# The gate's two weight loads cut into 120 and 8 partitions, in a one-core linear-attention and highway kernel

## The chip, the core and the metric

The kernel runs on one core of a Trainium2 chip. The metric is the device time of one execution in microseconds (us). A time shown for a kernel is the median of its runs. A profile is one execution recorded by the hardware profiler; its "span" is the part from the first to the last recorded instruction.

## What is computed

```python
# q, k, v: (8, 8, 576, 64) f32; w_h, w_t: (512, 512) f32; b_t: (512,) f32
q_s = exp(q - max) / sum            # softmax over the 64 of a head
k_s = exp(k - max) / sum            # softmax over the 576 positions
kv  = einsum('bhsd,bhse->bhde', k_s, v)
x   = einsum('bhsd,bhde->bhse', q_s, kv)   # then (8, 8, 576, 64) -> (4608, 512)
H = maximum(x @ w_h, 0)
T = 1 / (1 + exp(-(x @ w_t + b_t)))        # the gate
out = T * H + (1 - T) * x
```

The output is 4608 x 512 in f32. `w_t` is what is called the gate's weights here.

## The kernel before

**Stages.** For each of the eight batches the kernel loads k, v and q (1152 KB each), takes exponentials on ScalarE (ACT; L252 for k, L301 and L306 for q), casts v to f16 (L258, on GpSimd, ACT or VectorE), and multiplies k by v on TensorE (PE, L268). The result, divided by its row sums (L280, L286), stays in SBUF as weights. q is transposed on PE (L318, L323), copied back (L332) and multiplied by these weights (L352); VectorE (DVE) divides by the sums (L361, L367), which gives a tile x of 128 tokens by 512. There are 36 such tiles. Each is transposed (L375, L382) and multiplied by both weight matrices, four products of 128x512 each: with w_t into the gate's bank (L402) and with w_h (L410). Tanh on ACT (L424, L426), a maximum on DVE (L430), and two or three operations on GpSimd (POOL) or DVE (L441, L442, L444, L462) give the output, which is stored in pieces of 128 to 512 KB (L470, L478, L482).

**The order** is written out by hand: `ORDER`, a list of some 680 steps. A step's name says what it does and for which batch or tile; a letter after the colon picks the engine. Each engine runs its instructions in the order in which the steps issue them. Near the change the list has these loads, in this order, all on the queue of SyncE (SP): `w_h_0`, `w_h_2`, `w_t_2`, `w_t_0`, `k_1_2`, `v_1_2`, `q_1_0`, `k_1_0`, `v_1_0`, `q_1_4`, `q_2_0`, `k_2_0`, `v_2_0`, `q_3_0`. The number after the letter is the batch; the last number is the column group from which the piece starts (for w_t_2 and w_t_0 it names the half of the matrix).

**A weight load** (`load_w`, L207 to L210) brings half a matrix: 128 partitions with two rows of 512 f32 each, 4096 bytes per partition and 512 KB in all. w_h's halves are lessened by an identity on POOL (L225) and cast on ACT (L231). w_t's halves are cast on POOL (`wt_cast`, L221), w_t_2 first and w_t_0 after it. A product with w_t (L402) needs both halves.

**The queue.** A transfer of the program is spread over the core's 16 DMA engines; each engine works through its share of the transfers in the order of issue. The program has eight semaphores for transfers, taken in turn: a transfer is issued only once the eighth transfer before it has landed. A landing counts when every engine that carries a part has reported.

The lines that a load of the weights is made of:

```python
T[f"w{w}{c}"] = op.tile([P, 2, DM], FP32, tag="o32", name=f"w32{w}_{c}")
nc.sync.dma_start(T[f"w{w}{c}"], src.rearrange("(c p r) n -> c p r n", p=P, r=2)[c // 2])
...
copy(w16["t"][:, c:c + 2], T[f"wt{c}"])        # wt_cast, on POOL here
```

Of the kernel before, what the change touches and what calls it, by code (L numbers as in the profile page):

```python
# [65 lines left out]
def kernel(  # L66
# [10 lines left out]
    nc = tc.nc  # L77
    B, H, S, D = q.shape
    DM = H * D
    P = 128  # L80
# [36 lines left out]
    T = {}  # L117
# [89 lines left out]
    def load_w(e, w, c):  # L207
        src = dict(t=moe_w_t, h=moe_w_h)[w]
        T[f"w{w}{c}"] = op.tile([P, 2, DM], FP32, tag="o32", name=f"w32{w}_{c}")
        nc.sync.dma_start(T[f"w{w}{c}"], src.rearrange("(c p r) n -> c p r n", p=P, r=2)[c // 2])  # L210

    def load_b(e, r):
        nc.scalar.dma_start(b32[r:r + 1], moe_b_t.rearrange("(o n) -> o n", o=1))
# [250 lines left out]
    def st(e, i, h):  # L464
# [20 lines left out]
    does = dict(  # L485
        setuppool=setup_pool, setupdve=setup_dve, bsplit=bsplit, fill=fill,
        k=load_kv("k"), v=load_kv("v"), q=load_q, w=load_w, b=load_b, bp=bp, bc=bc,
        wtc=wt_cast, whc=wh_cast, whd=wh_less_identity, ek=ek, vc=vc, kv=kv, kr=kr, kn=kn, eq=eq, qt=qt, qc=qc,
        xu=xu, rs=rs, x=x, xt=xt, xe=xe, bw=bw, mt=mt, mh=mh, th=th, dd=dd, uu=uu, oo=oo, st=st)
# [35 lines left out]
```

## Time and profile before

| | |
|---|---|
| median of three runs | 119.56 us (119.36 to 119.63) |
| the profiled execution's own time | 119.67 us |
| its span | 117.6 us, 3461 instructions |
| PE busy | 110.6 us (94% of the span) |
| DVE, ACT, POOL busy | 94.3, 92.3, 91.9 us (80%, 78%, 78%) |
| DMA | 40.06 MB in 22083 packets, mean 341 GB/s |
| the chain that ended last, by engine | PE 69%, DMA 17%, DVE 8% |
| w_t loads, issue to landing | 2 x 512 KB, 11.2 us each |

Matmuls are pipelined, so a busy PE is not one at its peak. The chain that ended last is followed back from the last instruction: at each step to what released it, or to the instruction before it on its engine. A share of DMA in it means that the engines waited for transfers at that place. Besides the instructions the trace holds, for each transfer, the time at which each DMA engine's report arrived (called marks below: 16 for a transfer over 16 engines), and every DMA packet with its start, duration and size; it doesn't say which DMA engine a mark or a packet belongs to.

### The profile page before, as it was taken

The numbers are of one execution on the slowest core, as the hardware profiler recorded it, in microseconds if no ns is written. First come the engines' busy times: TensorE is split into PE (matmuls) and PEld (weight loads), VectorE is DVE, ScalarE is ACT, GpSimd is POOL, SyncE is SP. The second block draws the span as 40 slices with busy tenths as digits, with TensorE's granted clock in tenths as the row PEclk, the third lists the DMA queues.
The fourth block names the chain that finished last, engine by engine and source line by source line (L and its number), as shares of the span: only waits on it lengthen the run. The fifth ranks groups of instructions, "written<-read, shape, count | busy, mean of one in ns | idle before, by whom it ended". The sixth has DMA issues, their size and how long they took to land.

```text
span 117.6 us, 3461 instructions
## 1 busy us (share of the span) xinstructions
PE 110.6 (94%) x1371; PEld 63.6 (54%) x1371; DVE 94.3 (80%) x223; ACT 92.3 (78%) x130; POOL 91.9 (78%) x103
## 2 busy tenths in 40 slices
PE   5999867989999999999999999999999999999991
PEld 1354443535655666556655566666666655554450
DVE  5654685588769899997899999889989898988870
ACT  4375481798999999799999999996998987774520
POOL 5022237299999999999999999899999789996860
PEclk9999999999999999999999999999999999999999
DMA  2999999999999999999999999999999977971595
GB/s 46 393 392 380 408 396 385 378 375 384 394 389 390 389 391 362 374 355 390 389 375 383 381 363 361 395 374 380 406 403 363 279 235 180 301 283 56 210 364 173
DMA packets 22083, 40.06 MB, mean 341 GB/s; under 512 B 3250, under 2 KB 9650, under 8 KB 22068
## 3 DMA queue, kind: packets, MB, share of 16 engines
q1 hardware_dynamic: 21920, 39.72, 94.8%
q8 instruction: 10, 0.16, 0.6%
q10 hardware_dynamic: 148, 0.14, 0.4%
q14 instruction: 5, 0.04, 0.1%
HBM read 30.41 MB, written 9.44 MB: 339 GB/s over the span
## 4 chain that ended last, share of the span: by engine, by line
PE 69%; DMA 17%; DVE 8%; SPq 2%; ACT 1%; issue 1%; DVEq 0%
PE gps L410 23%; PE tps L402 22%; DMA q<-in_q_dram 11%; PE xu L352 6%; DMA v<-in_v_dram 6%; PE turned L375 5%; PE kv L268 4%; DVE x L367 4%; PE qps L323 2%; PE qps L318 2%; SPq L183 2%; PE turned L167 2%; DVE d L430 2%; ACT qe L306 1%; DVE rs L361 1%
## 5 line engine op out<-in xcount | busy, mean ns | idle before, releaser
L462 POOL TENSOR_TENSOR o<-u,x 128x512 f32<-128x512 f16 (+1 forms) x36 | 40.7, 1144 | 3.7 <-DVE u L444 2.8
L402 PE MATMUL tps<-w16t,xT 128*128 128x512 f16 (+1 forms) x148 | 36.3, 373 | 0.8 <-POOL w16t L221 0.8
L410 PE MATMUL gps<-w16h,xT 128*128 128x512 f16 x144 | 36.3, 379 | 0.0
L367 DVE TENSOR_TENSOR x<-xu,rs 128x512 f16<-128x512 f32 (+1 forms) x39 | 25.2, 649 | 2.8
L442 POOL TENSOR_TENSOR u<-g,d 128x512 f16<-128x512 f16 x21 | 24.3, 1157 | 2.5 <-DVE rs L361 0.9
L430 DVE SCALAR_TENSOR_TENSOR d<-x,gps 128x512 f16<-128x512 f16 x36 | 24.2, 678 | 1.7 <-PE gps L410 1.6
L252 ACT ACTIVATE ek<-k 128x576 f16<-128x576 f32 (+2 forms) x15 | 18.0, 1222 | 2.5 <-DMA k<-in_k_dram 2.5
L402 PEld LDWEIGHTS <-xT 128*128 128x128 f16 x148 | 13.4, 98 | 12.1 <-issue 1.1
L410 PEld LDWEIGHTS <-xT 128*128 128x128 f16 x144 | 12.8, 98 | 11.4 <-DVE xT L382 0.5
L390 ACT COPY tps<-ball 128x512 f32<-128x512 f32 x28 | 16.3, 592 | 2.4 <-DVE u L444 2.1
L258 POOL CAST v<-v 128x1152 f16<-128x1152 f32 (+1 forms) x10 | 9.5, 953 | 10.4 <-DMA v<-in_v_dram 9.9
L375 PE MATMUL turned<-idh,x 128*128 128x128 f16 x144 | 14.3, 220 | 1.0 <-DVE x L367 1.0
L352 PE MATMUL xu<-kvb,eq 128*128 128x130 f16 (+1 forms) x160 | 14.8, 224 | 0.5 <-DVE eq L332 0.2
L167 PE MATMUL turned<-blank 128*128 128x512 f16 x44 | 12.5, 431 | 1.3 <-POOL blank L149 1.3
L352 PEld LDWEIGHTS <-eq 128*128 128x128 f16 (+1 forms) x160 | 10.2, 100 | 6.5 <-DVE x L367 1.3
L424 ACT ACTIVATE th<-tps 128x512 f16<-128x512 f32 x21 | 12.3, 592 | 1.6 <-PE tps L402 1.6
L375 PEld LDWEIGHTS <-x 128*128 128x128 f16 x144 | 10.1, 98 | 6.5 <-DVE x L367 2.6
L441 POOL TENSOR_SCALAR g<-th 128x512 f16<-128x512 f16 x21 | 13.1, 622 | 0.2 <-ACT th L424 0.2
L382 DVE COPY xT<-turned 128x512 f16<-128x512 f16 (+1 forms) x27 | 10.8, 399 | 2.8 <-PE turned L375 2.5
L306 ACT ACTIVATE qe<-q 128x1024 f16<-128x1024 f32 (+2 forms) x8 | 9.2, 1160 | 4.3 <-DMA q<-in_q_dram 4.1
L426 ACT ACTIVATE tps<-tps 128x512 f32<-128x512 f32 (+1 forms) x16 | 8.9, 556 | 2.9 <-PE tps L402 2.7
L444 DVE SCALAR_TENSOR_TENSOR u<-tps,d 128x512 f16<-128x512 f32 (+1 forms) x15 | 10.0, 669 | 0.8 <-ACT tps L426 0.2
(48 smaller groups left out, 114.6 us busy)
## 6 DMA issues: line engine op xcount, KB each, us to landing
k<-in_k_dram SPq DMA_DIRECT2D x6, 1152.0 KB, 11.6
v<-in_v_dram SPq DMA_DIRECT2D x6, 1152.0 KB, 14.4
out_dram<-o SPq DMA_DIRECT2D x23, 256.0 KB, 6.3
q<-in_q_dram SPq DMA_DIRECT2D x10, 512.0 KB, 9.5
out_dram<-o SPq DMA_DIRECT2D x6, 512.0 KB, 5.5
k<-in_k_dram SPq DMA_DIRECT2D x4, 576.0 KB, 11.9
q<-in_q_dram SPq DMA_DIRECT2D x2, 1152.0 KB, 15.6
q<-in_q_dram SPq DMA_DIRECT2D x2, 640.0 KB, 10.5
```

The source lines that it names most:

```text
L167: nc.tensor.matmul(spare, blank[:, 0:P], blank, start=True, stop=True, skip_group_check=True)
L252: nc.scalar.activation(t[:, :, c:c + n].rearrange("p j c d -> p c j d"), T[f"k32{b}"][:, c:c + n].rearrange("p c (j d) -> p c j d", j=NJ), ...
L352: nc.tensor.matmul(dst, turned_q(b, jp, n), kvb[b % NKV][:, hh, kk], start=True, stop=True, skip_group_check=True)
L367: nc.vector.tensor_mul(t[:, k0:k1], sums(i, k)[:, :, :, 0:64], T[f"rs{i}_{k}"][:, 0:k1 - k0].unsqueeze(3).to_broadcast([P, k1 - k0, 4, D]))
L375: nc.tensor.matmul(t[:, n], T[f"x{i}"][:, n0 + n % 2:n0 + 2 * P:2], idh, is_transpose=True, start=True, stop=True, skip_group_check=True)
L390: nc.scalar.copy(t[:, cs], ball[:, cs])
L402: nc.tensor.matmul(T[gate(i, k)][:, cs], T[f"xT{i}"][:, n], w16["t"][:, n, cs], start=False, stop=(n == parts[-1] and not first), skip_gro ...
L410: nc.tensor.matmul(t, T[f"xT{i}"][:, n], w16["h"][:, n], start=(first and n == parts[0]), stop=(n == parts[-1] and not (first and len(part ...
L430: nc.vector.scalar_tensor_tensor(t, T[f"x{i}"], -0.5, T[f"gps{i}"], op0=ALU.mult, op1=ALU.max)
L441: nc.gpsimd.tensor_scalar(g, T[f"th{i}"], 1.0, 1.0, op0=ALU.add, op1=ALU.mult)
L442: nc.gpsimd.tensor_mul(t, g, T[f"d{i}"])
L462: eng.tensor_add(t[:, cs], T[f"u{i}_{h}"][:, cs], T[f"x{i}"][:, cs])
```

## The change

`load_w` issues each load of w_t as two transfers to the same tile: one of partitions 0 to 119 and one of partitions 120 to 127. The loads of w_h stay whole. The tile, its consumers and `ORDER` are the same; two transfers are added to SP's queue, so that each later transfer takes the semaphore two places further on. Each cast of w_t waits for two transfers.

```diff
     def load_w(e, w, c):
         src = dict(t=moe_w_t, h=moe_w_h)[w]
         T[f"w{w}{c}"] = op.tile([P, 2, DM], FP32, tag="o32", name=f"w32{w}_{c}")
-        nc.sync.dma_start(T[f"w{w}{c}"], src.rearrange("(c p r) n -> c p r n", p=P, r=2)[c // 2])
+        rows = src.rearrange("(c p r) n -> c p r n", p=P, r=2)[c // 2]
+        for part in (slice(0, 120), slice(120, P)) if w == "t" else (slice(0, P),):
+            nc.sync.dma_start(T[f"w{w}{c}"][part], rows[part])
```

## The prediction

> **What bounds the kernel now.** I read the slices and queues first.
>
> ```profile
> DMA  2999999999999999999999999999999977971595
> ...
> q1 hardware_dynamic: 21920, 39.72, 94.8%
> q8 instruction: 10, 0.16, 0.6%
> ```
>
> The DMA engines are full from the fourth microsecond to about 90 us, so a load lands when the engines get to it, not when it is issued. The q8 row is PE's own instructions: ten fetches of 16 KB; 0.6% of 16 engines' 117.6 us is 1.1 us for each, and each is one packet on one engine. Next, the waits and the chain:
>
> ```profile
> ACT qe L306 <- DMA q<-in_q_dram: 4.1, 4, 1.9
> ...
> POOL w16t L221 <- DMA w32t<-in_moe_w_t_dram: 1.9, 2, 1.6
> ...
> PE tps L402 <- POOL w16t L221: 0.8, 1, 0.8
> ```
>
> ```profile
> 3.79 7.00 DMA v<-in_v_dram
> 10.81 12.67 DMA q<-in_q_dram
> ...
> 23.50 1.06 ACT qe L306
> 24.56 0.05 issue
> 24.61 0.62 PE qps L323 x8
> ```
>
> Up to q_1_0's landing at 23.47 transfers set the end; from 24.6 the chain is PE, with DVE in two stretches, to the end. So an early landing before 23.5 pays, if no later landing takes it back. The marks show what lands last (last three of 16, us):
>
> ```
> w_h_2  15.05 15.06 15.15     k_1_2  19.10 19.22 20.45     q_2_0  30.02 31.24 31.38
> w_t_2  16.33 16.43 17.64     q_1_0  22.11 22.22 23.47     v_2_0  36.80 37.24 37.39
> w_t_0  17.60 17.70 18.95     q_1_4  26.93 27.04 28.26
> ```
>
> One engine falls behind in w_t_2 and stays 1.2 to 1.25 us behind the next. A q8 packet starts at 15.15 and takes 1.10 us: call its engine **the late one**. The fetch at 26.95 makes a second engine late, from q_2_0 on. The last of the others (16.43, 22.22) is the one that carried the one-row bias loads: the second bias row stood in its queue from 3.74 to 4.44, and one engine alone ended the transfer around it 0.7 us later than the rest.
>
> **The change part by part.** *Price of a row.* A 4096-byte packet takes 0.16 us around 15 us. 128 rows on 16 engines are 8 rows each, 1.28 us; w_h_2's first mark to w_t_2's is 1.25. How 120 rows are shared out no trace here shows. Nearest to the row "8 on each of 16" is 8 on each of 15, which leaves one engine out; I take that. The other bound is 15 rows on each of 8 engines. The 8 rows are one each on 8 engines, at most one row on any of them: 0.16 us per load, 0.33 for both with their marks (none, for an engine that gets none). The engine left out saves 16 rows, 2.56 us, more than the 1.54 us by which the late one missed its own slot (17.64 against 16.10).
>
> [...]
>
> *New landings, if the late engine is the one left out.* The bias engine, with its extra rows, is last: w_t_2 at 16.43 + 0.17 = 16.60 (17.64 now), w_t_0 at 17.70 + 0.33 = 18.03 (18.95), k_1_2 19.55 (20.45), q_1_0 22.22 + 0.33 = 22.55 (23.47): 0.92 earlier.
>
> *PE up to 31 us.*
>
> ```profile
> 17.69 1.04 POOL L221 CAST w16t<-w32t 128x1024 f16<-128x1024 f32 x1 [1.59 <-DMA w32t<-in_moe_w_t_dram]
> 19.00 1.04 POOL L221 CAST w16t<-w32t 128x1024 f16<-128x1024 f32 x1 [0.27 <-DMA w32t<-in_moe_w_t_dram]
> ```
>
> ```profile
> 18.24 1.03 PE L410 MATMUL gps<-w16h,xT 128*128 128x512 f16 x4
> 20.09 1.89 PE L402 MATMUL tps<-w16t,xT 128*128 128x512 f16 x8 [0.83 <-POOL w16t L221]
> ```
>
> The second cast would run from 18.08 to 19.12; PE is free at 19.27 (18.24 + 1.03), so the gate's first products start there instead of at 20.09: 0.82 gained, the wait of 0.8 above. The exponential of q_1_0 then follows 22.55 instead of 23.47, and PE's transposes 0.92 before 24.61. PE carries 0.92 onwards.
>
> *What takes it back.* q_2_0 and v_2_0 land with the second late engine, which nothing relieves: 31.38 and 37.39 stay.
>
> ```profile
> 31.40 2.12 ACT L306 ACTIVATE qe<-q 128x2304 f16<-128x2304 f32 x1
> 33.43 1.07 ACT L424 ACTIVATE th<-tps 128x512 f16<-128x512 f32 x2
> 34.38 1.11 ACT L390 COPY tps<-ball 128x512 f32<-128x512 f32 x2
> 35.42 2.13 ACT L252 ACTIVATE ek<-k 128x2304 f16<-128x2304 f32 x1
> 37.44 1.14 ACT L258 CAST v<-v 128x1152 f16<-128x1152 f32 x1
> ```
>
> ```profile
> 37.51 1.15 POOL L258 CAST v<-v 128x1152 f16<-128x1152 f32 x1
> ```
>
> ACT was free at 31.26 and starts at 31.40, behind the landing; from there it has no gap. The casts of v_2_0 end at 38.58 (ACT) and 38.66 (POOL) whatever came before, and PE's k-by-v products of batch 2 need both. They start at 38.98 in the chain (38.91 in PE's own rows). With 0.05 for the handover, as from the cast's end 20.04 to 20.09, they can't start before 38.71: **0.27 us is left** of 0.92. The next such place is v_3_0: its casts end at 47.69, the products start at 48.03, 0.34 less the 0.05 is 0.29, enough. After that no landing stands in the chain.
>
> *Costs at nothing.* SP issues two more transfers, 0.33 us each by L210's rows, and each transfer behind them waits for a landing two places later: q_1_0 issues after w_h_0's landing at 13.88, not at 10.81; k_1_2 at 10.8, not 8.54. Behind them on SP stand only later loads. The cover is the backlog: q_1_0's share starts on the engines no earlier than 19.6 (v_1_2's first mark, 20.10, less some 0.5 from an engine's last packet to its mark), 5.7 us after its issue, while the first load of the program had its first packet 1.1 us after issue. Without that cover each microsecond of late issue would be one of landing. Each cast waits for two transfers: one semaphore more, 0 to 0.1 us, hidden before PE's 19.27 (0.15 of room).
>
> *Sum.* The profiled execution's own 119.67 (117.6 span and 2.07 around it) would become 119.40; the median shown lies 0.11 lower, so 119.56 - 0.27 = **119.29 us**.
>
> **The rivals.** The trace doesn't number engines, so which one is late decides. For the forecast: the late engine isn't the bias engine, which took the 16.43 mark; each of the fetches up to 53.3 (five) hits another engine, and none hits the bias engine as far as the marks can be followed. One after the other is the simplest such order. [...] Against it: a walk may start anywhere, and any of 15 engines fits the mark.
>
> *R1, slower.* The late engine is one of the eight that get a row more. Place: q_1_0's last mark, 23.47 + 0.33 = 23.80, and w_t_0's, 18.95 + 0.33, so PE starts both the gate's products and the transposes 0.33 later, and the later landings (31.24 + 0.33 = 31.57) don't give it back. 119.89 us. It decides as soon as the late engine carries any of the 8 rows. [...] In this trace no engine lags but after a fetch.
>
> *R2, no effect.* The late engine is one of the others that keep 8 rows: 17.64, 18.95 and 23.47 stay and the extra rows hide in 1.2 us of lag. 119.56.
>
> *R3, eaten.* The late engine is relieved, but the second late one is among the eight: v_2_0 at 37.72, casts to 38.99, products at 39.04 against 38.98. 119.62.
>
> *R4, the split doesn't do what it says.* 15 rows on 8 engines are 2.4 us for each load instead of 1.28: 1.12 twice, and the row more, 2.57 on 22.22 is 24.79, 1.3 later; on the late engine 2.6. Some 2 us, 121.56.
>
> **How the numbers follow.** Forecast 0.45, R1 0.22, R2 0.18, R3 0.11, R4 0.04. 0.2% is 0.24 us, about what a measurement of this kernel can tell from no change. The forecast has bounds of 0 and -0.92 and lies near the line: 0.30 of its 0.45 faster, 0.15 same. R1: 0.18 slower, 0.04 same. R2: 0.14 same, 0.02 to each side. R3: 0.08 same, 0.03 slower. R4 slower. Faster 0.32, same 0.41, slower 0.27. The range goes from 119.00 (0.56 gained, half-way between 0.27 and 0.92 and a little less) to 119.95 (R1 and 0.06); R4 and the outer parts of the others are outside, under 0.2. Alone, the forecast's own range is 119.00 to 119.50.
>
> **What would show it.** Right: fewer than 16 marks of data for a 120-row load, last mark of w_t_2 near 16.6 and of q_1_0 near 22.55, the gate's first products at 19.3, the exponential of q_2_0 still at 31.4, and the k-by-v products of batch 2 at 38.7. R1 would show q_1_0 at 23.8, R2 at 23.47, R3 the products at 39.0, R4 the first mark of w_t_0 after 18.5. Wrong altogether would be a gap in the DMA slices before 31 us, from SP's later issues.

## The result

The changed kernel takes **122.86 us** (median of 4 runs, 122.33 to 123.15) against 119.50 us for the kernel before in the same rounds (119.36 to 119.63): a ratio of 1.0276, 95% interval 1.0237 to 1.0316. It is slower by 3.4 us; the forecast was 119.29 and its range ended at 119.95. The profiled execution took 122.72 us with a span of 120.9 (119.67 and 117.6 before). Two executions of one experiment below, the 60, 60 and 8 split, were disturbed (123.6 and 123.7 us) and are left out of its figures. All line numbers from L210 on are two higher than before: the casts of w_t are L223, the gate's products L404.

The page of the changed kernel, three rows by slices of 3.0 us (the granted clock of PE, the busy share of the DMA engines, and what they moved):

```profile
PEclk9999999769999999999999999999999999999999
DMA  2999999999999999999999999999999957970595
GB/s 51 395 395 383 377 232 249 372 385 378 385 394 388 398 380 378 362 365 384 383 384 371 393 358 372 386 371 379 399 406 353 283 196 199 299 285 7 220 381 173
```

The GB/s row of the kernel before, in slices of 2.9 us:

```profile
GB/s 46 393 392 380 408 396 385 378 375 384 394 389 390 389 391 362 374 355 390 389 375 383 381 363 361 395 374 380 406 403 363 279 235 180 301 283 56 210 364 173
```

The DMA row has a 9 in each slice from the second to the 32nd, up to 96 us: the engines do not run dry. But in the sixth and seventh slice, 15 to 21 us, busy engines move 232 and 249 GB/s; before they moved 396 and 385. That is where the pieces of w_t are loaded. The same traffic is slower, and a row of busy shares cannot show it.

The waits of the changed kernel, in us in total, times and the longest:

```profile
POOL w16t L223 <- DMA w32t<-in_moe_w_t_dram: 4.1, 2, 2.6
...
PE tps L404 <- POOL w16t L223: 3.2, 1, 3.2
```

The casts now wait 4.1 us for w_t (1.9 before), and PE waits 3.2 us for the second cast (0.8 before). The casts on POOL and the products on PE in order of time:

```profile
19.29 1.04 POOL L223 CAST w16t<-w32t 128x1024 f16<-128x1024 f32 x1 [2.63 <-DMA w32t<-in_moe_w_t_dram]
21.75 1.04 POOL L223 CAST w16t<-w32t 128x1024 f16<-128x1024 f32 x1 [1.42 <-DMA w32t<-in_moe_w_t_dram]
```

```profile
18.61 1.03 PE L412 MATMUL gps<-w16h,xT 128*128 128x512 f16 x4
22.84 3.49 PE L404 MATMUL tps<-w16t,xT 128*128 128x512 f16 x8 [3.21 <-POOL w16t L223]
```

The first products of the gate start at 22.84 (20.09 before), and the eight take 3.49 us instead of 1.89: behind the long wait PE's granted clock is 0.5 from 22.96 to 26.37 us (a mean of 0.7 and 0.6 in the eighth and ninth slice of the PEclk row), and the products follow one another every 0.43 us instead of 0.216. The group's row has it too, 37.9 us busy and a mean of 386 ns (36.3 and 373 in the kernel before, whose clock stays full):

```profile
L404 PE MATMUL tps<-w16t,xT 128*128 128x512 f16 (+1 forms) x148 | 37.9, 386 | 3.2 <-POOL w16t L223 3.2
```

And the chain that ended last, by engine and then its part from 3 to 30 us:

```profile
PE 56%; DMA 15%; ACT 11%; POOL 8%; DVE 3%; SPq 2%; issue 1%; DVEq 0%; POOLq 0%
...
3.25 6.74 DMA k<-in_k_dram
10.00 11.63 DMA w32t<-in_moe_w_t_dram
21.75 1.05 POOL w16t L223
22.84 3.49 PE tps L404 x8
26.33 0.30 PE turned L377 x4
26.63 0.88 PE gps L412 x4
...
27.54 0.69 DVE d L432
28.22 0.09 DVE rz L282
...
28.37 1.16 POOL u L444
```

Before, it went through q_1_0's landing and ACT to PE at 24.6; now it goes through the landing of w_t. Instruction by instruction, PE in the changed kernel stands 2.75 us behind before at the first gate product, 4.43 at 22 to 23 us (of before), 3.64 from 26 to 60, and 3.43 from 80 us to the end. Some 0.8 us is given back at 24.6, where PE waited 0.57 us for q_1_0 before and does not wait now, and 0.2 later. The rest stays. Behind 22 us the chain holds no transfer: its two loads make 18.4 us, the whole 15% of DMA, and what follows is work of PE, DVE, POOL and ACT with hardly a gap. The loads that follow are late too, since they stand behind the slow packets in the same queues: the last mark of q_1_0 is 25.86 (23.47 before), of q_2_0 33.95 (31.38).

Packets and marks come straight from the trace. The 256 packets of 4096 bytes that load w_t last as follows:

```
               150-180 ns  180-220  220-260  260-300  300-340  over 340   mean
before                254        0        0        0        0         2    164
after                  36       40       37       41       47        55    273
```

### The profile page after: what moved, and what is told of

The parts are those of the page before. It is cut to its first block, busy times and chain, and to the rows that moved or that the text cites. A ratio compares the mean times of both kernels' runs of the same rounds, so it can differ in the third digit from the quotient of the medians.

```text
span 120.9 us, 3465 instructions
## 1 busy us (share of the span) xinstructions
PE 112.0 (93%) x1371; PEld 64.1 (53%) x1371; DVE 94.5 (78%) x223; ACT 92.0 (76%) x130; POOL 91.7 (76%) x103
## 4 chain that ended last, share of the span: by engine, by line
PE 56%; DMA 15%; ACT 11%; POOL 8%; DVE 3%; SPq 2%; issue 1%; DVEq 0%; POOLq 0%
PE tps L404 20%; PE gps L412 19%; DMA w32t<-in_moe_w_t_dram 10%; DMA k<-in_k_dram 6%; PE xu L354 5%; PE turned L377 5%; ACT ek L254 3%; PE kv L270 3%; POOL u L444 3%; POOL o L464 3%; PE qps L320 2%; PE turned L167 2%; ACT v L260 2%; ACT tps L392 2%; ACT qe L308 2%; SPq L183 2%
## 5 line engine op out<-in xcount | busy, mean ns | idle before, releaser
L404 PE MATMUL tps<-w16t,xT 128*128 128x512 f16 (+1 forms) x148 | 37.9, 386 | 3.2 <-POOL w16t L223 3.2
L412 PE MATMUL gps<-w16h,xT 128*128 128x512 f16 x144 | 36.3, 379 | 0.0
L404 PEld LDWEIGHTS <-xT 128*128 128x128 f16 x148 | 13.7, 100 | 15.3 <-issue 5.1
```

The lines of the kernel that those rows point to most:

```text
L404: nc.tensor.matmul(T[gate(i, k)][:, cs], T[f"xT{i}"][:, n], w16["t"][:, n, cs], start=False, stop=(n == parts[-1] and not first), skip_gro ...
L412: nc.tensor.matmul(t, T[f"xT{i}"][:, n], w16["h"][:, n], start=(first and n == parts[0]), stop=(n == parts[-1] and not (first and len(part ...
```

## The experiments

The theories, from the two traces. **P**, place: what counts is where in SBUF the packets of a piece go; the pieces make several DMA engines write into the same group of partitions. **E**: a transfer over 15 engines is slow as such. **H**: the order of the rows in the source memory counts. **S** and **Q**: the small piece as such, or the place of the extra transfers in the queue. **C**: of the 3.4 us a good part is PE's clock, which is at 0.5 behind the wait.

Each diff below is against the changed kernel unless it says otherwise, and its lines are in `load_w`; lines that only allocate a tile or register a step are not shown. The kernel before had medians of 119.53 in the rounds of the first four kernels, 119.79 for the next four, 119.75 for the 60, 60 and 8 split and the repeat of the changed kernel, and 119.66 for every fourth and every eighth partition. The mean duration of w_t's packets and the marks are of the profiled execution.

**Two halves of 64 neighbouring partitions.**

```diff
-        for part in (slice(0, 120), slice(120, P)) if w == "t" else (slice(0, P),):
+        for part in (slice(0, 64), slice(64, P)) if w == "t" else (slice(0, P),):
```

> Each w_t load as partitions 0 to 63 and 64 to 127. All 16 engines carry both pieces, 4 rows each. Theory P (destinations): a piece of neighbouring partitions, as it is shared out, puts several engines on the same group of SBUF partitions at once, and their packets slow each other. P expects rows as slow as in the changed kernel (some 0.3 us instead of 0.16), w_t_0 landing at 21 to 22 us and 122 to 123 us in all. Theory E (engine count): it is the 15 engines, or their uneven load, that is slow; E expects packets of 0.16 us, w_t_0 landing near 18.9 and 119.5 us. Theory S (the small piece): single rows on 8 engines hold up the queue; S expects 119.5 too. [...]

121.75 us (121.16 to 122.13), ratio 1.017 (1.0132 to 1.0209); packets 269 ns; w_t_0's last mark 21.04. All 16 engines take part, and the packets are as slow as in the change. E alone can't be the cause, nor the small piece. The time lies a little under the 122 to 123 that P expected; the halves lose 2.2 us where the change loses 3.4.

**The same halves, but even and odd partitions.**

```diff
-        for part in (slice(0, 120), slice(120, P)) if w == "t" else (slice(0, P),):
+        for part in (slice(0, P, 2), slice(1, P, 2)) if w == "t" else (slice(0, P),):
```

> Each w_t load as its 64 even and its 64 odd partitions. All 16 engines, 4 rows each, two transfers as in e1. The wide q loads of the kernel before have the same stride of two and took 1.47 to 1.50 us for 512 KB, as the whole-partition load q_1_0 did (1.49). P expects little or no slowing (every piece reaches all of the partitions' groups): w_t_0 near 19 to 19.5, 119.4 to 120. E and S expect 119.5. A time like the changed kernel's, 122 to 123, would say that it is the number of transfers, or of rows per engine, and not the destinations.

119.58 us (118.94 to 120.41), ratio 0.9995 (0.9963 to 1.0026); packets 164 ns; w_t_0 18.96, q_1_0 23.47, the marks of before to 0.01. The GB/s rows of the two kernels, halves first:

```profile
GB/s 47 382 396 378 385 241 283 372 384 377 390 392 389 393 385 375 364 363 382 387 384 368 393 359 369 386 383 374 404 400 387 272 200 180 280 327 12 216 381 174
```

```profile
GB/s 47 388 396 379 405 399 383 377 377 387 389 391 392 388 392 359 375 354 389 390 374 383 379 365 361 396 373 380 406 403 372 333 158 219 327 231 39 216 369 178
```

Two transfers of 64 rows each in both, issued in the same places: 241 and 283 GB/s against 399 and 383 in the same slices. The second transfer, its issue and the casts' second wait cost nothing that can be measured (the interval ends at 0.3 us).

**112 and 16 partitions.**

```diff
-        for part in (slice(0, 120), slice(120, P)) if w == "t" else (slice(0, P),):
+        for part in (slice(0, 112), slice(112, P)) if w == "t" else (slice(0, P),):
```

> Each w_t load as 112 and 16 partitions. All 16 engines carry both, 7 rows and 1 row each, so that no engine has more or less work than before. E expects no loss: 119.5. S expects little (the small piece is spread over 16). P expects most of the loss of the changed kernel, since seven neighbouring rows for each engine again cross the groups: packets of 0.25 to 0.3 us in the larger piece and 121 to 123 us.

121.69 us (120.86 to 122.56), ratio 1.0171 (1.0113 to 1.0229); packets 250 ns. Again 16 engines, again slow.

**The whole load, and the 8 rows once more** to a tile that nobody reads.

```diff
-        for part in (slice(0, 120), slice(120, P)) if w == "t" else (slice(0, P),):
-            nc.sync.dma_start(T[f"w{w}{c}"][part], rows[part])
+        nc.sync.dma_start(T[f"w{w}{c}"], rows)
+        if w == "t":
+            nc.sync.dma_start(scratch[120:P, c // 2], rows[120:P])
```

> Each w_t load whole, and behind it a second transfer of the 8 last rows, to a tile that nothing reads. S expects most of the loss: w_t_0 late by 1 us or more and over 121 us, and so would a cost of the two added places in the queue. P and E expect the price of the rows alone: at most 0.33 us on eight of the engines, 119.5 to 119.9.

120.32 us (119.96 to 121.36), ratio 1.0075 (1.0039 to 1.011). Neither expectation held, 119.5 to 119.9 or over 121. The 8 rows alone cost 0.8 us, more than the 0.33 of their bytes; the mean packet is 182 ns, and 50 of the 272 last over 180 ns, where before had 2 of 256.

**The same with the 8 rows four partitions apart** (the diff is against the kernel just above).

```diff
-            nc.sync.dma_start(scratch[120:P, c // 2], rows[120:P])
+            nc.sync.dma_start(scratch[0:32:4, c // 2], rows[120:P])
```

> e3 (each w_t load whole, and 8 rows more to a tile that nothing reads), with the 8 rows now to partitions 0, 4, ... 28 instead of 120 to 127. P expects that the 8 rows go to eight groups of partitions and disturb little: the price of rows, 0 to 0.33 us, 119.5 to 119.9, against 120.3 in e3. Theory Q (a place in the queue or the second transfer as such costs 0.8) expects 120.1 to 120.5 again.

119.61 us (119.34 to 119.85), ratio 0.9992 (0.9959 to 1.0024); 270 of 272 packets between 150 and 180 ns. The same rows of the source and the same number of bytes and transfers: the 0.8 us were their destinations. S and Q fall. The forecast's 0.33 for the added rows is more than enough for these destinations, and too little for those of the change.

**Source and destination crossed**, one execution of each. Here the rows of the gate's matrix land in other places, so its products are of a matrix with moved rows. Only the added lines of the diffs are shown; they stand for w_t's loads alone.

```diff
+            nc.sync.dma_start(T[f"w{w}{c}"][0:64], rows[0:P:2])
+            nc.sync.dma_start(T[f"w{w}{c}"][64:P], rows[1:P:2])
```

> Destinations as in e1 (partitions 0 to 63, then 64 to 127), sources as in e2 (every other row of the matrix): the gate's weights lie in the wrong partitions, so the gate is that of a matrix with its rows moved. Theory P (destinations) expects packets as slow as e1's, a mean of 250 to 280 ns, w_t_0's last mark past 20.5 and 121 to 122.5 us. Theory H (sources: engines that read neighbouring rows of the matrix hinder each other in memory) expects e2: 164 ns, 19.0, 119.5 us.

```diff
+            nc.sync.dma_start(T[f"w{w}{c}"][0:P:2], rows[0:64])
+            nc.sync.dma_start(T[f"w{w}{c}"][1:P:2], rows[64:P])
```

> The reverse: destinations every other partition as in e2, sources in neighbouring halves as in e1; the gate's matrix has its rows moved here too. P expects e2: a mean of 164 ns for a packet and 119.5 us. H expects e1: 270 ns, 121 to 122.5 us.

Destination halves from alternate source rows: 121.94 us, packets 275 ns. Alternate destinations from source halves: 119.91 us, packets 164 ns. In the GB/s rows, the halves first:

```profile
GB/s 51 391 394 379 387 232 282 371 388 377 389 390 389 387 392 374 362 364 380 392 384 365 395 357 369 386 381 374 403 401 383 320 172 222 315 251 29 219 363 175
```

```profile
GB/s 42 359 395 381 405 397 387 376 376 384 392 391 389 386 391 364 370 359 386 394 371 384 377 365 363 398 370 382 404 400 366 310 164 225 325 237 37 209 376 178
```

The slow slices (232 and 282) go with the destination, whatever the source. H falls.

**The changed kernel with PE kept busy** through its wait: 14 products of a zero tile are added into an open bank, behind the product with w_h that ends at 19.9 us.

```diff
- ... mh_3_0 qc_0_2:A ...
+ ... mh_3_0 z_14 qc_0_2:A ...
+    def zeros(e, n):
+        for _ in range(n):
+            nc.tensor.matmul(T[gate(1, 0)], blank[:, 0:P], blank, start=False, stop=False, skip_group_check=True)
```

> The changed kernel with 14 products of zeros added into the gate's bank of tile 1 before its first products, so that PE doesn't stand still while it waits for the cast; the sums are the same. Theory C (the wait of 3.2 us makes the granted clock fall, and the gate's first eight products run at half speed, 3.5 us instead of 1.7) expects the granted clock at 0.99 or more, these products at 1.7 to 1.9 us, and 122.86 less 0.4 to 1.2: 121.7 to 122.4 us. If the landings alone set the end, 122.7 to 123 stays.

A miss: 123.08 us (122.93 to 123.33), ratio 1.0289 (1.0246 to 1.0331). The clock did stay up (a mean of 1.0), and the timeline of PE shows the products:

```profile
19.72 3.18 PE L173 MATMUL tps<-blank 128*128 128x512 f16 x14
23.39 1.89 PE L408 MATMUL tps<-w16t,xT 128*128 128x512 f16 x8 [0.49 <-POOL w16t L227]
```

The eight products take 1.89 us again, and from 31 to 60 us this execution is 0.73 ahead of the changed kernel, though its first gate product starts 0.55 later. Its chain goes through q_1_0's landing, as before the change, and reaches PE's transposes 2.94 us later than there (24.61):

```profile
14.11 12.30 DMA q<-in_q_dram
...
26.44 1.07 ACT qe L312
...
27.55 0.62 PE qps L329 x8
```

At 69 us it falls back, from 0.73 ahead to 0.27 behind:

```profile
68.14 0.70 PE L274 MATMUL kv<-v,ek 64*64 64x65 f16 x62
69.64 0.28 PE L274 MATMUL kv<-v,ek 64*64 64x65 f16 x10 [0.80 <-issue]
```

PE stops for 0.80 us in the middle of one batch's k-by-v products, 62 of 72 done, and waits for nothing that the profile names. A fetch of PE's instructions ran from 67.24 to 68.32, just before. The 14 products are 28 more instructions, each with its weight load as the 1371 of both on the page of the changed kernel, so the fetches fall at other places of the program; in the changed kernel the fetch nearest to this place (67.90 to 69.01) stops nothing. That the fetch is the cause was not tried. So C holds in part: the fallen clock is worth some 0.7 us at 60 us, and this way of keeping it up costs more than that later. The four executions of the changed kernel itself point the same way: the one whose mean granted clock was 1.000 had a span of 120.5 us, the three at 0.986 had 120.7 to 120.9. By these two comparisons the clock is 0.2 to 0.7 of the 3.4 us.

**60, 60 and 8 partitions**, the 120 as even and odd.

```diff
-        for part in (slice(0, 120), slice(120, P)) if w == "t" else (slice(0, P),):
+        for part in (slice(0, 120, 2), slice(1, 120, 2), slice(120, P)) if w == "t" else (slice(0, P),):
```

> The 120 rows of the change as two transfers of 60, even and odd partitions of the first 120, and the last 8 as before in a transfer of their own: still one engine left out of 15, but every engine's four rows lie on alternate partitions, as in the split into even and odd that took no longer than the whole load. Theory P (the slow packets come from pieces of neighbouring partitions that several engines write at once): the packets of the 60 rows near 164 ns; the 8 neighbouring rows may still cost what the 8 extra rows cost, 0.8 us; so a mean below 200 ns, last mark of w_t_0 at 18.9 to 19.9, time 119.3 to 120.4. If 15 engines instead of 16 are slow as such: packets of 250 ns or more and 122 us or more. If the forecast was right in its mechanism and only the packets' price spoilt it (the engine left out is the late one): last mark of w_t_2 near 16.6 and q_1_0 near 22.55 in the traced execution, and about 0.3 us under the kernel before, 119.3; if the late engine is not the one that is left out, nothing is gained.

A miss: 121.98 us (121.35 to 122.12), ratio 1.016 (1.0107 to 1.0213), packets 238 ns. The partitions of each piece alternate, and it is slow. That 15 engines are slow as such, for which 250 ns and 122 us or more were expected, would fit this run almost as well; it does not separate the two, and the slow kernels that speak against E are those with 16 engines. "Pieces of neighbouring partitions" was the wrong wording of P. What would fit is that engines can get in each other's way also when the rows of a piece alternate.

This gives a wider theory, **P2**: what counts is how many engines write to one group of partitions at the same moment. Which partitions make a group, and which engine writes which row, no trace here shows; there P2 rests on the author's assumption. The last two kernels test it with steps of four and of eight partitions.

**Every fourth partition, four transfers of 32 rows.**

```diff
-        for part in (slice(0, 120), slice(120, P)) if w == "t" else (slice(0, P),):
+        for part in [slice(i, P, 4) for i in range(4)] if w == "t" else (slice(0, P),):
```

> Each load of the gate's weights in four transfers of 32 rows, every fourth partition. [...] With two rows for each of 16 engines. [...]

Two outcomes were expected, by how the rows of a piece are dealt to the engines: 164 ns a packet and 119.2 to 120.3 us if the engines keep apart, 250 to 300 ns and about 121.7 us if two of them meet. If the number of transfers is what costs, the time was to be more than 0.5 us above the even and odd split with either. The packets are as fast as whole (mean 165 ns, 244 of 256 between 150 and 180). The time is not: 120.99 us (120.31 to 121.89), ratio 1.0109 (1.0054 to 1.0163). Stretches of 1 us show why (busy time of each engine with its instructions in brackets, and at the end PE's clock, the DMA share and GB/s):

```profile
16.00:17.00 1.00, 0.74 (x7) 0.41 (x7) 0.79 (x4) 0.78 (x2) 0.64 (x2) 1.00 0.80 307
17.00:18.00 1.00, 0.43 (x8) 0.43 (x9) 0.85 (x2) 0.99 (x2) 0.00 (x0) 1.00 0.54 155
18.00:19.00 1.00, 1.00 (x10) 0.53 (x8) 0.42 (x1) 0.00 (x0) 0.82 (x1) 1.00 0.86 170
19.00:20.00 1.00, 1.00 (x9) 0.52 (x8) 0.89 (x4) 0.37 (x1) 0.76 (x2) 1.00 1.00 382
```

Here the DMA share does fall, to 0.54, with fast packets: the engines run dry. SP issues the eight pieces from 7.57 to 16.18 us, because from the fourth on most wait for a landing, and k_1_2 follows at 16.22 (10.76 in the changed kernel). Six more issues cost some 0.9 us on q_1_0's landing (24.40, before 23.47). The packets are those of the first outcome, the time is not: at 1.0109 of the kernel before, against 0.9995 for the even and odd split, the number of transfers does cost here, by their issues.

**Every eighth partition, eight transfers of 16 rows**, for w_t_2 alone; w_t_0 whole; one execution.

```diff
-        for part in (slice(0, 120), slice(120, P)) if w == "t" else (slice(0, P),):
+        for part in [slice(i, P, 8) for i in range(8)] if (w, c) == ("t", 2) else (slice(0, P),):
```

> Only the first load of the gate's weights (w_t_2) in eight transfers of 16 rows, every eighth partition; w_t_0 whole. [...] P2: the 128 packets of w_t_2 take 250 to 300 ns, those of w_t_0 164, so a mean of some 210 to 230 over both; w_t_0's last mark 1 us later than whole, near 20, time 120.3 to 121.5 in one look. If it is neighbouring partitions that cost: 164 ns throughout and 119.3 to 120.3.

122.42 us. Rows eight partitions apart are slow: the packets that load w_t, 32 at a time in order of start, have these medians (the first group, from 14.3 us, is half of w_h; the fifth is half of w_t_0, the rest behind it all w_t_0):

```
164  366  364  236  212  166  159  159  159  ns
```

That excludes "neighbours". It agrees with P2 if engines meet at a step of eight partitions, which was assumed and is not shown. A single row for each engine is not the reason either: the 8 spread rows above were such a transfer, and fast. The slow medians, 364 and 366 ns, lie above the 250 to 300 that P2 expected. The time is 1 us above what was expected, since the later issues again left a hole (a 5 and 118 GB/s in the sixth slice):

```profile
DMA  2999958999999999999999999999999898970594
GB/s 43 382 393 379 386 118 310 385 389 372 389 393 388 391 388 383 356 366 379 386 389 362 394 362 373 378 385 372 399 403 368 265 262 225 288 299 36 217 361 169
```

**The changed kernel once more**, unaltered, for the late engine.

> The changed kernel once more, unaltered, for one thing: which engine PE's instruction fetch at 15.6 us makes late. In the first trace it was one of the eight that carry a row of the 8-row piece (its mark came last of those, 19.16 against 18.06). If the engine is fixed, the same again. If it changes from one execution to the next, the late mark may be among the 120-row load's alone, or the engine left out may show a gap of about 1.1 us in its chain of 2304-byte packets. The packets of the gate's load again 250 to 290 ns in either case, and a time of 122.3 to 123.2 us.

124.80 us in this one execution, above the 122.3 to 123.2 expected, with packets of 289 ns, a fetch of 1.33 us, and PE's clock at 0.5 for 6.8 us (3.4 in the first trace). Only its marks and packets are used here. In the first trace of the changed kernel the last mark of w_t_2's 8-row piece stands alone, so the late engine was one of the eight; here it does not, and the 120-row piece has the lone mark:

```
          120 rows, last three     8 rows, last three
first     17.66  17.98  18.67      17.95  18.06  19.16
again     18.13  18.25  20.14      17.78  18.36  18.37
```

The same program, the same fetch, another engine. In neither was it the engine that is left out: that one goes on to k_1_2 alone, and its packets of 2304 bytes follow one another through the whole of the fetch (15.62 to 16.85, and 16.43 to 17.76) without a gap of its length.

None of these kernels beats the one before; even and odd halves and the spread 8 rows equal it.

## Why the prediction was wrong

**The step that failed is the price of a row.** The forecast took 0.16 us per 4096-byte packet from whole loads and used it for pieces. In the pieces the same packet took 0.27 us in the mean. Sixteen rows an engine at 0.109 more are 1.74 us, and the rates give the same: 1.05 MB take 4.37 us at 240 GB/s and 2.65 at 396. The slowing also reached the load that runs beside the pieces: the first 256 packets of 2304 bytes, as many as k_1_2 has, took 157 ns in the mean instead of 97, another 0.96 us an engine. The packets of w_h_2, ahead of the pieces, did not change (163 ns in both). Together that is 2.70 us, and it is what the landings show: the median of q_1_0's marks moved by 2.66 us (21.99 to 24.65) and its last by 2.39, w_t_0's last by 2.68 (18.95 to 21.63). The forecast had a gain of 0.92 in this place.

*How 120 rows are shared out* was right: 15 marks of data, and one engine ahead of the others by 3.3 us in the next load (18.04, then 21.35). The 0.33 us for the added rows was too small: the same 8 rows to the same partitions, beside whole loads, cost 0.8 us, and nothing measurable only when they were spread. That the bias engine gets a row of each 8-row piece, as the forecast's 16.60 and 18.03 have it, no run shows, since no mark names its engine; the last marks came at 19.16 for w_t_2 and 21.63 for w_t_0.

*New landings* failed twice. The late engine was not the one left out in either trace, and it differs between executions, so the forecast's 0.45 rested on a place that the trace of before could not fix. Even where the premise had held, w_t_2 at 16.60 was out of reach at 0.27 us a row.

*What takes it back* did not act: q_2_0 and v_2_0 were expected to stay because a second engine was late in them, but the whole queue had moved, 2.57 us on q_2_0, and no later landing stood in the chain. A landing is fixed by a late engine only as long as all the others stay in front of it.

*Costs at nothing* held for the two issues (even and odd halves, spread rows), but the argument for it was too generous. The cover was read at q_1_0's share, 5.7 us; six more issues, with k_1_2's at 16.22 instead of 10.76, already left a hole at the pieces themselves and at k_1_2.

*What would show it*: a gap in the DMA slices was named as the sign of "wrong altogether". There was none; the sign was in the row below it, GB/s.

*The rivals.* R1's premise held in the profiled execution (the late engine among the eight), with 0.33 us of the 3.4. R4 was nearest in time, 121.56, by a mechanism that did not occur (15 rows on 8 engines); its sign, the first mark of w_t_0 after 18.5, showed (19.16) for the other reason. No rival had an engine at its usual work and its packets slower. Nor had one the clock: a wait of 3.2 us on PE, which the forecast would have priced at its length, also made the eight products behind it last 1.6 us longer, of which 0.2 to 0.7 us are left at the end by the two comparisons above.

What is shown, and what is not: that destinations decide is shown by the crossed kernels and by the two placings of 8 rows; that it is not the distance between the partitions, by the fourth and eighth ones. That it is the number of engines that write to one group of partitions at the same moment is P2. No run here contradicts it, and none shows it: which partitions make a group, and how the rows of a piece are dealt to the engines, was assumed, since no packet names its engine or its partition. Whether 15 engines without such meetings would cost anything was not tried, so it stays open how the 1.1 us or so that the change loses beyond the halves divide between engine count, the eight rows and the clock.

## What to carry to other kernels

A duration of a packet belongs to the shape of its transfer: price a split load by packets of a load that was split in the same way, and if there is none, let the range hold twice the packet (364 against 164 ns here). Read GB/s next to the busy share of the DMA engines, because an engine that is held up counts as busy (a 9 in the busy row at 232 and 249 GB/s here). And a long wait on PE can have a second price, the products behind it at a lower clock (3.49 us instead of 1.89 at 0.5 here, behind 3.2 us).

## What the runs showed of the hardware that was not expected

- The destination's partitions alone change a 4096-byte packet from 164 to 275 ns, with 16 engines, the same bytes and the same number of transfers; 8 rows of 4 KB on neighbouring partitions, twice, cost 0.8 us of a 119.5 us kernel, and nothing when they are four apart.
- An instruction fetch of 16 KB is one packet of 0.88 to 1.24 us in the first trace of the changed kernel and of 1.33 in its repeat, and meets another DMA engine there. It is taken to be PE's, whose products and weight loads are 2742 of the 3465 instructions.
- PE's clock fell to 0.5 behind a wait of 3.2 us (0.43 us from product to product, 0.216 before) and behind one of 2.4 (halves, mean of the gate's products 381 ns), but not behind one of 2.7 (112 and 16, mean 374 ns). The trace's clock records have it at 0.5 for 3.41 us, from 22.96 and from 22.97, and for 6.83 us in the repeat. Executions of one program differ as well: the mean granted clock was 0.986 in three of four of the changed kernel, and in one of four of the halves and of 112 and 16. The length of the wait alone does not decide.
